# Token-major attention scores with undivided exponentials, in a kernel of pooled attention and a gated feed-forward

## The chip, the cores and the metric

The kernel runs on one core of one Trainium2 chip. The metric is device time in microseconds (us) of one execution; lower is better. The kernel before took 1031.86 us, the median of three runs (1031.65 to 1032.02).

## What is computed

Four images, each with 12288 query tokens of 128 channels and a kv map of 384 x 32 pixels. The kv map is averaged over 4 x 4 pixels to 768 rows and multiplied by `w_sr`; the result serves as key and as value.

```
kv_pool = kv.reshape(B, H//4, 4, W//4, 4, C).mean(axis=(2, 4))
k = v = kv_pool.reshape(B, -1, C) @ w_sr            # 768 rows an image
a = softmax(q @ k.T / sqrt(C))
x = (a @ v).reshape(B*N, C)                         # 49152 tokens, 128 channels
out = (maximum(x @ w_gate, 0) * (x @ w_val)) @ w_out   # d_ff = 1536
```

The feed-forward has no bias and its gate is a relu, so a positive factor on a token's row of x goes through it squared. The attention may therefore leave out its division by the sum of exponentials, if the output row is multiplied by the squared inverse of the sum.

## The kernel before, in words

The tokens are cut into 96 tiles of 512 (`T`), 24 to an image. A tile passes through five stages, each in another iteration of the outer loop (line 610), whose index is k:

- Scores (`scores`, line 290), tile k: for each of the six chunks of 128 keys, one matmul with the keys stationary and 512 tokens moving gives a bank of scores, keys on partitions. ScalarE takes its exponential into `aT` (line 295).
- Values (`values`, line 297), tile k - 1: for each chunk and each block of 128 tokens, `aT` is stationary and the values, with one more column of constants, are moving: 24 matmuls of 129 columns (line 305). The extra column is the sum of exponentials, scaled. VectorE takes its reciprocal (line 313) and multiplies (line 321); the result `x16` has tokens on partitions, and a DMA transpose (`x_turn`, line 329) turns it into `xT`, channels on partitions.
- Feed-forward, tile k - 3 (`LAG`): for each of the twelve blocks of 128 features, a value product (`value_proj`, line 374, copied to `val` by ScalarE, line 378) and a gate product (`gate_proj`, line 385). VectorE takes the relu of the gate and multiplies it by `val` in one instruction (line 388) into `hT`.
- Output product, tile k - 4 (`out_proj`, line 407): twelve matmuls into one bank. VectorE transposes that bank in blocks of 32 x 32 (line 415), GpSimd scales by a constant (line 423), and four DMAs of 64 KB store it from SP's queue (line 634).

All inner work is interleaved by a loop over 12 steps, in which each step issues one output product, one value product, a score chunk or four value matmuls, and one gate product. PSUM is one pool of eight banks taken in turn (line 85).

The first four tiles (`LEAD`) go another way, in an opening whose order is written out by hand (`OPENING`, `ENGINES`): their values are stationary, their exponentials stay undivided, and their outputs are scaled by squared inverse sums (line 421) from a matmul with ones.

Beside this, for images 2 to 4, SP loads kv in the last half of the image before, GpSimd pools it (lines 194 to 202), VectorE transposes blocks, SP places them through DRAM, TensorE projects them (line 259), and a DMA transpose gives the values (line 284). Queries are loaded by GpSimd's queue with a cast to fp16 (line 114) and turned by a DMA transpose of 2048 columns for four tiles (line 124).

Of the kernel before, what the change touches and what calls it, by code (L numbers as in the profile page):

```python
# [16 lines left out]
def kernel(  # L17
# [41 lines left out]
    LEAD = GRP  # L59
    qk_scale = 1.0 / math.sqrt(C)  # L60
# [5 lines left out]
        a0:p b0:p p0:p kvT1:a key1:a val1:a a2:p kvT2:a kvT3:a kvT4:a key4:a cast0:p qT1:a  # L66
        cast2:a cast4:p cast5:p xT3:a
    """.split())
    OPENING = """
        T1.0 T1.1 cast1 a0 T1.3 b0 T1.2 kvT1 p0 cast2 pj1 T0.3 cast3 key1 cast0 T0.p kvT0 qt2 a2  # L70
        gate22 W0 W1 cast4 qT4 wo cast5 qT5 qt1 vt1 qt3 qT2 pj0 T3.0 qT1 val1 S1.1 key0 qt0 S2.0
        S2.1 T3.1 V1.1 qT3 qT0 S1.0 S0.1 vt0 b2 val0 S3.1 S0.0 T3.2 V2.1 V0.1 T3.3 kvT3 S3.0
        V1.0 pj3 c2 p2 T2.p kvT2 key3 V0.0 S1.3 vt3 pj2 S3.3 key2 val3 S2.3 V2.0 V1.3 a4 S0.3 a5
        S1.2 S3.2 S2.2 T4.2 p4 b5 T4.p vt2 V0.3 V2.3 T4.3 val2 kvT4 S0.2 c5 p5 V2.2 pj4 V1.2
        T5.p key4 kvT5 S1.4 vt4 S0.4 val4 pj5 S2.4 V0.2 V1.4 key5 S0.5 V0.4 vt5 val5 S3.4 S2.5
        V2.4 S1.5 V0.5 S3.5 U0 xT0 V1.5 v0.2 U1 xT1 R v0.4 V2.5 xT2 v0.5 v0.3 g0.2 v0.0 V3.3
        g0.4 V3.4 v0.1 V3.5 v0.6 g0.3 g0.5 v0.7 v0.10 g0.0 v0.11 g0.10 V3.2 S4.5 S4.2 g0.1 V3.0
        v0.8 S4.0 g0.6 g0.11 v0.9 g0.8 V3.1 xT3 g0.7 S4.4 g0.9
    """.split()
    SUMS = [{"a": [0, 1], "b": ["s", 2]}, {}, {"a": [0, 1], "b": ["s", 2], "c": ["s", 3]}, {}, {"a": [0, 1]}, {"a": [0, 1], "b": ["s", 2], "c": ["s", 3]}]  # L80
# [4 lines left out]
    psum = ctx.enter_context(tc.tile_pool(name="psum", bufs=8, space=bass.MemoryType.PSUM))  # L85

    def bank(shape, dtype=FP32):
        return psum.tile(shape, dtype, tag="bank", name="bank_ps")
# [38 lines left out]
    def q_load_pair(i):  # L127
        q32 = work.tile([128, 2, NS, C], FP32, tag="q32", bufs=2, name="q32")
        nc.sync.dma_start(  # L129
            q32, q[0, i * T : (i + 2) * T, :].rearrange("(p i s) c -> p i s c", i=2, s=NS)  # L130
        )
        for n in range(2):
            q32s[i + n] = q32[:, n]

    def q_load_tile(i):
        q32 = work.tile([128, T], FP32, tag="o_t", bufs=2, name="q32_late")
        nc.sync.dma_start(
            q32, q[0, i * T : (i + 1) * T, :].rearrange("(t j s) c -> j t (s c)", j=4, s=NS)
        )
        q32s[i] = q32.rearrange("p (s c) -> p s c", s=NS)  # L140
# [17 lines left out]
    def q_turned(i):  # L158
        copy_on(f"qT{i}", qTs[0][:, i * NS : (i + 1) * NS, :], q_banks.pop(i))
# [16 lines left out]
    def kv_load(b, pair, lines=range(r), queues=(nc.sync,)):  # L176
        if (b, pair) not in kv_in:
            kv_in[b, pair] = work.tile([128, r, 2, r, C], FP32, tag="kv_in", bufs=3, name="kv_in")
# [4 lines left out]
        for dh in lines:  # L183
            queues[dh % len(queues)].dma_start(  # L184
                parts[:, dh].rearrange("p h dw c -> p (h dw c)"), rows[dh]
            )
# [3 lines left out]
    def pool_pixels(eng, b, pair, h):  # L190
        parts = kv_in[b, pair]
        s2 = work.tile([128, 2, r, C], FP32, tag="kv_s2", bufs=1)
        for i in range(2):
            eng.tensor_tensor(s2[:, i], parts[:, 2 * i, h], parts[:, 2 * i + 1, h], op=ALU.add)  # L194
# [9 lines left out]
    def line(chunk, dh):  # L204
        return kv_in[0, chunk // 2][:, dh, chunk % 2]
# [26 lines left out]
    def turned(name, chunk):  # L232
        kvT = work.tile([128, 128], FP32, tag="kvT_chunk", bufs=3, name="kvT_chunk")
        copy_on(name, kvT, kv_Ts[chunk])
# [8 lines left out]
    def keep_keys(name, jc):  # L243
        pr, engine = key_ps.pop(jc), engine_of(name)
# [9 lines left out]
    def keep_chunk_values(name, jc):  # L254
        copy_on(name, kv16[:, 0, jc, C : 2 * C], value_ps.pop(jc))

    def project(b, pair):
        pr = bank([128, 4, 2, 32])
        nc.tensor.matmul(pr, w_sr_f32, kv_Ts.pop((b, pair)), start=True, stop=True)  # L259
        nc.vector.tensor_scalar(  # L260
            kv16[:, b, 2 * pair : 2 * pair + 2, 0:C].rearrange("c h (i p) -> c h i p", p=32),
            pr.rearrange("c i h p -> c h i p"), 1.0 / (r * r), None, op0=ALU.mult,
        )

    def turn_blocks(b, pair):

        blocks = work.tile([128, 4, 2, 32], FP32, tag="kv_blocks", bufs=2)
# [22 lines left out]
    def scores(k, jc):  # L290
        if k not in aTs:
            aTs[k] = work.tile([128, NJC, T], FP16, tag="aT", bufs=5, name="aT")
        s_ps = bank([128, T])
        nc.tensor.matmul(s_ps, kv16[:, k // NST, jc, 0:C], qT_of(k), start=True, stop=True)  # L294
        nc.scalar.activation(aTs[k][:, jc, :], s_ps, AF.Exp, scale=qk_scale)  # L295

    def values(k, jc, half):
        if jc == 0:
            x_banks[k, half] = bank([128, 2, C + 1])
            if half == 0:  # L300
                x16s[k] = work.tile([128, NS, C], FP16, tag="x16", bufs=3, name="x16")
        x_ps = x_banks[k, half]
        for i in range(2):
            s = 2 * half + i
            nc.tensor.matmul(  # L305
                x_ps[:, i, :], aTs[k][:, jc, s * 128 : (s + 1) * 128],
                kv16[:, k // NST, jc, C : 2 * C + 1],
                start=(jc == 0 and i == 0), stop=(jc == NJC - 1), skip_group_check=True,
            )

    def keep_sums(k, half):
        rinvs[k, half] = work.tile([128, 2, 1], FP32, tag="rinv", bufs=4, name="rinv")
        nc.vector.reciprocal(rinvs[k, half], x_banks[k, half][:, :, C : C + 1])  # L313

    def keep_values(k, half, engine=nc.vector):
        x_ps, rinv = x_banks.pop((k, half)), rinvs.pop((k, half))
        if engine is nc.scalar:
            for i in range(2):
                nc.scalar.mul(x16s[k][:, 2 * half + i, :], x_ps[:, i, 0:C], rinv[:, i])
        else:  # L320
            nc.vector.tensor_tensor(  # L321
                x16s[k][:, 2 * half : 2 * half + 2, :], x_ps[:, :, 0:C],
                rinv.to_broadcast([128, 2, C]), op=ALU.mult,
            )

    def x_turn(k):
        x16 = x16s.pop(k)
        xT = work.tile([128, NS, 128], FP16, tag="xT", bufs=5, name="xT")
        nc.sync.dma_start_transpose(xT, x16.rearrange("p s c -> p (s c)"))
        xTs[k] = xT.rearrange("c s p -> c (s p)")  # L330

# [12 lines left out]
    def lead_kept(name, k):  # L344
        xTs[k] = work.tile([128, NS, 128], FP16, tag="xT", bufs=5, name="xT").rearrange("c s p -> c (s p)")
        copy_on(name, xTs[k], x_banks.pop(k))
# [12 lines left out]
    def lead_scales():  # L359
        turned = work.tile([128, NS * 4, 32], FP32, tag="o_sb", bufs=3, name="sums_turned")  # L360
        nc.vector.transpose(turned.rearrange("p x m -> p (x m)"), x_banks.pop("sums"))
# [9 lines left out]

    def value_proj(k, fb):
        va_ps = bank([128, T])
        nc.tensor.matmul(  # L374
            va_ps, wv16[:, fb * 128 : (fb + 1) * 128], xTs[k], start=True, stop=True
        )
        val = work.tile([128, T], FP16, tag="val", bufs=6, name="val")
        nc.scalar.copy(val, va_ps)  # L378
        vals[k, fb] = val

    def gate_proj(k, fb):
        if k not in hTs:
            hTs[k] = work.tile([128, NFB, T], FP16, tag="hT", bufs=3, name="hT")
        g_ps = bank([128, T])
        nc.tensor.matmul(  # L385
            g_ps, wg16[:, fb * 128 : (fb + 1) * 128], xTs[k], start=True, stop=True
        )
        nc.vector.scalar_tensor_tensor(  # L388
            hTs[k][:, fb, :], g_ps, 0.0, vals.pop((k, fb)), op0=ALU.max, op1=ALU.mult
# [21 lines left out]
    def out_turn(k):  # L411
# [3 lines left out]
        nc.vector.transpose(o_t, o_banks.pop(k))  # L415
# [3 lines left out]
        if k < LEAD:  # L419
            scale = lead_scale[:, k].rearrange("t (s j o) -> t s j o", s=NS, o=1)  # L420
            nc.gpsimd.tensor_tensor(to, o_by, scale.to_broadcast([128, NS, 4, 32]), op=ALU.mult)  # L421
        else:
            nc.gpsimd.tensor_scalar(to, o_by, 1.0 / X_SCALE**2, None, op0=ALU.mult)  # L423
# [19 lines left out]
    def out_scale(k, engine, own, o_ps=None):  # L443
        if k not in o_sbs:
            o_sbs[k] = work.tile([128, NS, 128], FP32, tag="o_sb", bufs=3, name="o_sb")
        o_sb, o_ps = o_sbs[k][:, own], o_ps if o_ps is not None else o_banks[k]
        if engine is nc.scalar:
            nc.scalar.mul(o_sb, o_ps, 1.0 / X_SCALE**2)
        else:
            nc.vector.tensor_scalar(o_sb, o_ps, 1.0 / X_SCALE**2, None, op0=ALU.mult)  # L450
# [51 lines left out]
    nc.sync.dma_start(w_sr_f32, w_sr)  # L502
    q_load_pair(2)
    q_load_pair(0)
    kv_load(0, 1)
    kv_load(0, 2)
    q_load_tile(4)
    q_load_tile(5)
# [18 lines left out]
    fill(4)  # L527
# [4 lines left out]
    def open_step(word):  # L532
# [44 lines left out]
        elif head == "v":  # L577
            value_proj(*at)
        elif head == "g":
            gate_proj(*at)  # L580
        elif head == "W":
# [19 lines left out]
    for word in OPENING:  # L601
# [4 lines left out]
    out_moves, moves = [], []  # L606


    last = NT + LAG - 1
    for k in range(LEAD, last + 1):  # L610
# [10 lines left out]
        for step in range(NFB):  # L621
            kO, kF = k - LAG - 1, k - LAG
            half, i = divmod(step // 2, NJC // 2)
            if 0 <= kO:
                out_proj(kO, step)
                if step == NFB - 1 and kO < NT - 3:
                    out_moves = out_turn(kO)
                elif step == NFB - 1 and k < last:
                    out_scale(kO, nc.vector, slice(0, NS))
                    out_store(kO, slice(0, NS))  # L630
            if 2 <= step < 10:
                for _ in range(2):
                    if out_moves:
                        nc.sync.dma_start(*out_moves.pop())
            if kF < NT:
                value_proj(kF, step)
            if step % 2 == 0:
                if k < NT and (k, step // 2) not in done:
# [60 lines left out]
```

## Time and profile before

| | |
|---|---|
| median of three runs | 1031.86 us |
| the profiled execution's own time | 1031.71 us |
| its span in the profile | 1029.9 us |
| TensorE busy | 1023.6 us (99%), 6508 matmuls |
| VectorE, ScalarE busy | 909.3 us each (88%) |
| GpSimd busy | 288.0 us (28%) |
| DMA, hardware queue of SP and software queue of GpSimd | 38.1% and 11.5% of 16 engines' span |

The profile is of one execution. Its span leaves out 1.8 us around it that the run's time has. Busy time is the union of an engine's instructions, which overlap on TensorE and ScalarE; so a busy share near 100% says less than the distance between starts.

### The profile page before, as it was taken

The page shows a single profiled execution, that of the slowest core. Times are in us where ns is not written, and L with a number is a line of the kernel's source. Part 1 is how long each engine was busy: PE and PEld are TensorE (multiplying, and loading weights), DVE is VectorE, ACT ScalarE, POOL GpSimd, SP SyncE. Part 2 cuts the span into 40 slices and gives each one's busy share as a digit, 9 for nine tenths or more (in the row PEclk, how much of TensorE's full clock was granted, in tenths as well). Part 3 has the DMA queues.
Part 4 walks back from the last instruction along what each step waited for, and adds up shares of the span by engine and source line. Part 5 has one row for each costly group of instructions (what it writes and reads, how often), then busy time and mean ns, then how long its engine had stood idle before and what let it go on. Part 6 is the DMA issues. An engine that isn't in the chain of part 4 may idle for free.

```text
span 1029.9 us, 19910 instructions
## 1 busy us (share of the span) xinstructions
PE 1023.6 (99%) x6508; PEld 541.1 (53%) x6508; DVE 909.3 (88%) x1666; ACT 909.3 (88%) x1742; POOL 288.0 (28%) x311
## 2 busy tenths in 40 slices
PE   8999999999999999999999999999999999999998
PEld 5455555555555555555555555555555555555555
DVE  3889898998989898998889898989898888989898
ACT  5988888888888898888898888888888898888887
POOL 4402156511221124742112122664121211111110
PEclk9999999999999999999999999999999999999999
DMA  8936386362652657826345167572552433513122
GB/s 320 116 52 80 100 184 142 78 92 39 88 69 49 74 125 158 169 57 88 54 64 88 32 88 144 146 163 58 84 77 43 73 58 62 87 32 66 33 43 51
DMA packets 327807, 93.33 MB, mean 91 GB/s; under 512 B 307480, under 2 KB 320664, under 8 KB 327704
## 3 DMA queue, kind: packets, MB, share of 16 engines
q1 hardware_dynamic: 312584, 77.97, 38.1%
q0 software_dynamic: 14688, 12.98, 11.5%
q10 hardware_dynamic: 432, 1.11, 0.3%
q8 instruction: 51, 0.84, 0.3%
q14 instruction: 52, 0.43, 0.2%
HBM read 53.94 MB, written 26.35 MB: 78 GB/s over the span
## 4 chain that ended last, share of the span: by engine, by line
PE 98%; DMA 1%; SPq 0%; DVE 0%; issue 0%; ACT 0%; ACTq 0%
PE bank_ps L374 24%; PE bank_ps L385 24%; PE bank_ps L407 23%; PE bank_ps L305 12%; PE bank_ps L294 12%; DMA q<-in_q_dram 1%; PE bank_ps L393 1%; PE bank_ps L339 1%; PE bank_ps L259 0%; PE bank_ps L227 0%; PE bank_ps L241 0%; PE bank_ps L353 0%; SPq L184 0%; DVE q L98 0%; SPq L129 0%; SPq L502 0%
## 5 line engine op out<-in xcount | busy, mean ns | idle before, releaser
L388 DVE SCALAR_TENSOR_TENSOR hT<-bank_ps,val 128x512 f16<-128x512 f32 x1152 | 757.2, 686 | 90.5 <-ACT val L378 70.4
L378 ACT CAST val<-bank_ps 128x512 f16<-128x512 f32 x1152 | 677.6, 589 | 103.0 <-PE bank_ps L374 99.9
L374 PE MATMUL bank_ps<-xT,wv 128*128 128x512 f16 x1152 | 436.3, 379 | 0.0
L385 PE MATMUL bank_ps<-xT,wg 128*128 128x512 f16 x1152 | 436.3, 379 | 0.0
L407 PE MATMUL bank_ps<-hT,wo 128*128 128x512 f16 x1116 | 423.0, 379 | 0.0
L295 ACT ACTIVATE aT<-bank_ps 128x512 f16<-128x512 f32 x576 | 344.9, 603 | 1.6 <-PE bank_ps L294 1.6
L423 POOL TENSOR_SCALAR o_sb<-o_t 128x512 f32<-128x512 f32 x89 | 132.6, 1489 | 664.6 <-DVE rinv L313 633.3
L305 PEld LDWEIGHTS <-aT 128*128 128x128 f16 x2208 | 170.6, 98 | 130.2
L294 PE MATMUL bank_ps<-qT,kv 128*128 128x512 f16 x576 | 216.6, 379 | 0.0
L305 PE MATMUL bank_ps<-kv,aT 128*128 128x129 f16 x2208 | 215.3, 220 | 0.0
L374 PEld LDWEIGHTS <-wv 128*128 128x128 f16 x1152 | 112.7, 98 | 133.4 <-DMA xT<-x 0.4
L385 PEld LDWEIGHTS <-wg 128*128 128x128 f16 x1152 | 112.7, 98 | 67.9
L407 PEld LDWEIGHTS <-wo 128*128 128x128 f16 x1116 | 109.2, 98 | 66.0 <-issue 0.2
L294 PEld LDWEIGHTS <-kv 128*128 128x128 f16 x576 | 56.2, 98 | 66.8 <-DVE kv L248 0.6
L321 DVE TENSOR_TENSOR x<-bank_ps,rinv 128x256 f16<-128x256 f32 x184 | 78.1, 425 | 6.5
L415 DVE STREAM_TRANSPOSE o_t<-bank_ps 128x512 f32<-128x512 f32 x93 | 65.6, 706 | 0.0
L114 POOL DMA_DIRECT2D q<-in_q_dram x84 | 46.3, 558 | 0.4 <-ACT xT L96 0.4
L194 POOL TENSOR_TENSOR s<-kv_in 128x512 f32<-128x512 f32 x36 | 44.9, 1267 | 0.0
L313 DVE RECIPROCAL rinv<-bank_ps 128x2 f32<-128x2 f32 x184 | 26.7, 145 | 0.0
L196 POOL TENSOR_TENSOR s<-s 128x512 f32<-128x512 f32 x18 | 22.8, 1267 | 1.4
L198 POOL TENSOR_TENSOR c<-s 128x256 f32<-128x256 f32 x18 | 13.1, 727 | 1.4
L421 POOL TENSOR_TENSOR o_sb<-o_t,lead_scale 128x512 f32<-128x512 f32 x4 | 4.2, 1048 | 32.3 <-DVE rinv L313 16.2
(68 smaller groups left out, 131.5 us busy)
## 6 DMA issues: line engine op xcount, KB each, us to landing
kv_in<-in_kv_dram SPq DMA_DIRECT2D x46, 512.0 KB, 6.8
out_dram<-o_sb SPq DMA_DIRECT2D x353, 64.0 KB, 2.2
q<-in_q_dram POOLq DMA_DIRECT2D x84, 128.0 KB, 4.6
xT<-x SPq DMA_TRANSPOSE x92, 2.5
out_dram<-o_sb SPq DMA_DIRECT2D x80, 16.0 KB, 1.5
placed<-blocks SPq DMA_DIRECT2D x9, 128.0 KB, 2.7
kvT<-placed SPq DMA_DIRECT2D x36, 32.0 KB, 1.9
kv_in<-in_kv_dram ACTq DMA_DIRECT2D x2, 512.0 KB, 7.5
```

What stands on the lines that cost most here:

```text
L114: nc.gpsimd.dma_start(q16[32 * j : 32 * (j + 1)].rearrange("t (i s) c -> t i s c", i=GRP), rows[j])
L294: nc.tensor.matmul(s_ps, kv16[:, k // NST, jc, 0:C], qT_of(k), start=True, stop=True)
L295: nc.scalar.activation(aTs[k][:, jc, :], s_ps, AF.Exp, scale=qk_scale)
L305: nc.tensor.matmul(x_ps[:, i, :], aTs[k][:, jc, s * 128 : (s + 1) * 128], kv16[:, k // NST, jc, C : 2 * C + 1], start=(jc == 0 and i == 0) ...
L321: nc.vector.tensor_tensor(x16s[k][:, 2 * half : 2 * half + 2, :], x_ps[:, :, 0:C], rinv.to_broadcast([128, 2, C]), op=ALU.mult,)
L374: nc.tensor.matmul(va_ps, wv16[:, fb * 128 : (fb + 1) * 128], xTs[k], start=True, stop=True)
L378: nc.scalar.copy(val, va_ps)
L385: nc.tensor.matmul(g_ps, wg16[:, fb * 128 : (fb + 1) * 128], xTs[k], start=True, stop=True)
L388: nc.vector.scalar_tensor_tensor(hTs[k][:, fb, :], g_ps, 0.0, vals.pop((k, fb)), op0=ALU.max, op1=ALU.mult)
L407: nc.tensor.matmul(o_banks[k], wo16[:, fb, :], hTs[k][:, fb, :], start=fb == 0, stop=fb == NFB - 1)
L415: nc.vector.transpose(o_t, o_banks.pop(k))
L423: nc.gpsimd.tensor_scalar(to, o_by, 1.0 / X_SCALE**2, None, op0=ALU.mult)
```

## The change

From the fifth tile on, the scores are made token by token: a block of 128 queries is stationary and all 768 keys are moving, in two matmuls of 512 and 256 columns, into a tile of two banks (`wide`). One ScalarE instruction takes the exponential of 768 columns and sums the row (`accum_out`). SP turns each block by a DMA transpose of 768 columns into `aT`. Two iterations later (before: one) the values are stationary and `aT` moves: six matmuls of 512 columns give `xT` directly, which VectorE copies from the bank; there is no division, no `x16` and no x transpose. The row sums are inverted on VectorE and squared on GpSimd for two tiles at a time, spread over partitions by 16 small copies, and GpSimd multiplies the outputs by them in place of the constant.

```diff
+    def score_block(k, s):
+        ...
+        s_ps = s_banks[s] = wide.tile([128, 1024], FP32, tag="wide", name="wide_ps")
+        qT = qTs[k // GRP][:, k % GRP * NS + s, :]
+        for j0, j1 in ((0, 4), (4, NJC)):
+            nc.tensor.matmul(
+                s_ps[:, j0 * 128 : j1 * 128], qT, kv16[:, b, j0:j1, 0:C], start=True, stop=True
+            )
+    def exp_block(k, s):
+        nc.scalar.activation(
+            a16s[k][:, s, :], s_banks.pop(s)[:, 0:J], AF.Exp, scale=qk_scale,
+            accum_out=a_sums[k // 2][:, k % 2, s : s + 1],
+        )
+    def invert(k):
+        ...
+        nc.vector.reciprocal(inverse, a_sums.pop(k // 2))
+        ...
+        nc.gpsimd.tensor_tensor(square, inverse, inverse, op=ALU.mult)
+    def spread_scales(k, j):
+        ...
+        for b in range(4):
+            nc.gpsimd.tensor_copy(
+                to[32 * b : 32 * (b + 1), :, :, j], squares[k // 2][32 * j : 32 * (j + 1)]
+            )
+    def a_turn(k, s0, s1):
+        aT = aTs[k].rearrange("k j t -> k (j t)").rearrange("k (x p) -> k x p", p=128)
+        nc.sync.dma_start_transpose(
+            aT[:, s0 * NJC : s1 * NJC], a16s[k][:, s0:s1, :].rearrange("p s j -> p (s j)")
+        )
+    def values(k, jc):
+        ...
+        aT = aTs[k].rearrange("k j t -> k (j t)").rearrange("k (s j p) -> k j s p", s=NS, j=NJC)
+        nc.tensor.matmul(
+            x_banks[k], kv16[:, k // NST, jc, C : 2 * C], aT[:, jc],
+            start=first, stop=x_left[k] == 0,
+        )
+    def keep_values(k):
+        ...
+        nc.vector.tensor_copy(xTs[k], freed(x_banks.pop(k)))
```

The loop over 12 steps gives way to a written order. A letter is a kind of work, a number its block: s score block, e exponential and its transpose, x value matmul, k (in `kA`) the copy to `xT`, v and y the feed-forward's value product and its copy, g and h the gate product and the product into `hT`, o output product, `oT` the output's transpose and scaling, r the inversion, and tb, P, pk the kv work.

```diff
+    STEADY = """
+        v10 s0 o0 y10 e0 v1 y1 o1 o2 o3 v0 g1 s1 o4 v2 tb y0 v9 o5 o6 e1 h1 g0 g9 y2 g10
+        o7 s2 h0 y9 g2 h10 v7 o8 h9 o9 v3 o10 o11 h2 g7 v8 e2 x1 y7 g8 s3 r oT x5 y3 g3
+        y8 v6 x4 h7 x2 x0 v5 x3 v4 h8 e3 h3 y6 P g5 y5 v11 g11 kA pk g4 y4 h5 y11 g6 h6
+        h11 h4
+    """.split()
...
-        for step in range(NFB):
...
+        kO, kF, kV = k - LAG - 1, k - LAG, k - 2
+        for word in STEADY if k < last else LAST:
+            if head == "o":
+                out_proj(kO, n)
+                for queue in (nc.gpsimd, nc.sync):
+                    if out_moves and n >= 2:
+                        queue.dma_start(*out_moves.pop())
```

The same list holds in iterations that lack a stage: its words are then passed over. The last iteration has an order by block (`LAST`). Banks are named by hand: `bank` takes the one freed longest ago out of eight, and out of six from shortly before the opening's end; the other two become `wide`. The output DMAs are shared between GpSimd's queue and SP's.

The opening has another order and other engine choices; the scores of tile 4 that it held are no longer in it, the pair of query tiles 0 and 1 is loaded ahead of the pair 2 and 3, tiles 4 and 5 are loaded in four DMAs each, and three warming matmuls stand in place of four. Buffers of `kv_in` go from three to two, of `aT` from five to four, of `xT` from five to four; new are four of `a16`, which also hold the last kv lines of the first image.

## The prediction

> **What bounds the kernel now.** I began with the page's busy shares and its chain of waits, and went on to the groups of instructions with shapes kept apart, the timeline of single engines in the middle of the run, and the issue times of the DMA queue.
>
> ```profile
> PE 1023.6 (99%) x6508; PEld 541.1 (53%) x6508; DVE 909.3 (88%) x1666; ACT 909.3 (88%) x1742; POOL 288.0 (28%) x311
> ...
> PE 98%; DMA 1%; SPq 0%; DVE 0%; issue 0%; ACT 0%; ACTq 0%
> ```
>
> The chain that ended last is TensorE for 98%. A busy matmul row proves little, because matmuls overlap (379 ns each, though a new one starts every 216 ns). So the starts decide:
>
> ```profile
> 501.57 0.39 PE L305 MATMUL bank_ps<-kv,aT 128*128 128x129 f16 x4
> 501.80 0.38 PE L385 MATMUL bank_ps<-xT,wg 128*128 128x512 f16 x1
> ...
> 503.10 0.38 PE L374 MATMUL bank_ps<-xT,wv 128*128 128x512 f16 x1
> 503.31 0.39 PE L305 MATMUL bank_ps<-kv,aT 128*128 128x129 f16 x4
> ```
>
> Two groups of value products are 1.74 us apart, with seven 512-column matmuls between: 7 x 0.216 = 1.51, and the group of four 129-column ones fills the other 0.226 (56.5 ns each). No room is left. From 37.52 (first L407) to 1023.68 (last tile's output) the counted matmuls at these prices come to about 985.7 of 986.2 us. The middle is a TensorE stream without stalls, 10.42 us a tile. The others:
>
> ```profile
> L388 DVE SCALAR_TENSOR_TENSOR hT<-bank_ps,val 128x512 f16<-128x512 f32 x1152 | 757.2, 686 | 90.5 <-ACT val L378 70.4 <-PE bank_ps L374 1.5
> L378 ACT CAST val<-bank_ps 128x512 f16<-128x512 f32 x1152 | 677.6, 589 | 103.0 <-PE bank_ps L374 99.9 <-DVE o_t L415 0.4 <-DVE rinv L313 0.3
> L295 ACT ACTIVATE aT<-bank_ps 128x512 f16<-128x512 f32 x576 | 344.9, 603 | 1.6 <-PE bank_ps L294 1.6
> ```
>
> ```profile
> 499.17 0.59 ACT L378 CAST val<-bank_ps 128x512 f16<-128x512 f32 x1 [0.17 <-PE bank_ps L374]
> 499.66 0.60 ACT L295 ACTIVATE aT<-bank_ps 128x512 f16<-128x512 f32 x1
> 500.14 0.59 ACT L378 CAST val<-bank_ps 128x512 f16<-128x512 f32 x1
> 500.91 0.59 ACT L378 CAST val<-bank_ps 128x512 f16<-128x512 f32 x1 [0.17 <-PE bank_ps L374]
> ...
> 508.49 2.47 DVE L388 SCALAR_TENSOR_TENSOR hT<-bank_ps,val 128x512 f16<-128x512 f32 x4
> ```
>
> ScalarE starts a new evacuation every 0.487 us: 18 a tile are 8.77 us, and it waits for TensorE in the rest. VectorE starts one of the L388 products every 0.617: 7.40 a tile, with the transpose (0.63) and two normalisations (1.0) about 9.0. Both have under 1.7 us to spare.
>
> **What the Trainium skill says.** (1) "TensorE: Matmul & The Clock Gate", section "Wait — 56ns, not 53.3ns?": warm matmuls start N / 2.4 GHz + 2.5 ns apart, 215.7 ns at 512 columns. The trace agrees: 216, and 56.5 for 129 (56.3 by the formula). So 256 columns should take 109 ns. (2) "PSUM — Partial Sum Buffer", section "The four PSUM rules": an output fits one bank of 512 fp32. Hence a 768-column score block takes two matmuls and two banks. (3) "ScalarE: Activation LUTs", section "What ACT_TABLE_LOAD costs": 0.833 ns per element, neighbours overlapping by 93 ns. The trace shows 0.10 overlap. (4) "DMA: Bandwidth & Descriptors", section "Latency and other measured facts": 261 GB/s for transposes. This trace is slower (below), and its number is used.
>
> **The change part by part**, for the 92 tiles from the fifth on.
>
> TensorE. Scores: six of 512 columns (1.296 us) become four pairs of 512 + 256: 4 x (0.216 + 0.109) = 1.300. Values: 24 x 56.5 = 1.356 become 6 x 0.216 = 1.296. Net -0.056 a tile, and with the formula's bare 56.3 -0.050. For 92 tiles that is -4.6 to -5.2; I take **-5.0**. The period goes from 10.42 to 10.37. Weight loads drop from 66 to 50 a tile and lie beside running matmuls, as now.
>
> ScalarE. Twelve casts stay (5.84). Six exponentials (2.92) become four of 768 columns: 603 + 256 x 0.833 = 816 ns, less 0.116 overlap, 0.70 each, 2.80. No row here shows the new accumulated row sum. Bounds: 0 if it rides along, 0.30 if it is a further small instruction like the 202 ns ACTIVATE on one column (L512) with its overlap lost too. I take 0.2 each. Sum 9.44 of 10.37: hidden by TensorE, until the readout reaches (10.37 - 8.64) / 4 = 0.43.
>
> VectorE. Gone: two reciprocals and two L321 products (about 1.0). New: one xT cast like L98's 689 ns (0.62 in a row) and a small reciprocal per two tiles (0.07). Sum 8.72, 0.3 less, hidden.
>
> GpSimd. The output scaling goes from 1489 ns (L423) to the broadcast form, 1048 (L421). Added per two tiles: a square and 16 small copies (16 took 3.68 here). Two output DMAs a tile move here from SP at 0.56 each (L114's issue). Sum about 1.05 + 1.9 + 1.1 + 0.55 for q = 4.6, and 5.0 more in the 18 image tiles that pool kv: 9.6, still under a period. Its lateness is covered by two o_t buffers; without them VectorE's transpose would wait.
>
> SP and the DMA engines. The x transpose (512 columns, 1.21 us of issue) goes; four of 768 columns come.
>
> ```profile
> L329 SPq DMA_TRANSPOSE xT<-x x92: 1189/1213/3097, 57.6 to 1009.4; - x92
> ...
> L124 SPq DMA_TRANSPOSE qT<-q x22: 1912/3868/5914, 43.9 to 928.4; - x22
> ...
> 45.00:46.00 1.00, 1.00 (x6) 0.45 (x5) 1.00 (x3) 0.88 (x3) 0.00 (x0) 1.00 0.99 193
> 46.00:47.00 1.00, 1.00 (x6) 0.49 (x5) 1.00 (x2) 0.94 (x3) 0.00 (x0) 1.00 1.17 217
> ```
>
> Columns of the first two: issue time min/median/max in ns. The undisturbed 2048-column transpose took 1.91 us of issue and, in the windows from 43 to 48 (two shown; DMA share is the last but one number), 2.9 us of all 16 engines, 180 GB/s. Interpolated, 768 columns take 1.3 us of SP and 1.1 us of the engines. SP per tile: 4 x 1.3 + 2 outputs x 0.62 + qT 3.9 / 4 = 7.4 of 10.37; up to 5.5 more in alternate image tiles (kv loads, placing, value turns). DMA engines: today's queues took 38.1 + 11.5%, 511 us; less 92 x 0.78, plus 92 x 4.4: 844, 82%. What waits behind these: in SP's order each a_turn waits for its exponential, and outputs, qT and kv moves queue behind. The products need the result late: the last exponential stands at about 70% of iteration k, the first product at 60% of k + 2, nearly two periods (19 us) against a landing of 2.5 to 9 us. So all of this is costed at nothing; the cover is that distance.
>
> Banks. Two of eight now belong to one score block, refilled only after its exponential has read it; v and g products have four banks beside o and x. In STEADY 7, 9 and 11 matmuls (1.5 us or more) lie between one block and the next, against about 1.4 for the matmuls' end (0.4), one cast ahead in ScalarE's queue and the exponential with its readout: a refill should just find its banks read.
>
> Tiles that are not full. STEADY is laid for a whole tile. Iterations 4 and 5 carry no values: TensorE 9.08 us, but ScalarE 9.44, at least 0.37 lost in each. Iterations 96 to 98 have no scores, and o4 needs h4, VectorE's last product of the iteration before, only 14 words earlier. Following the words with the durations above I find 0.5 to 0.8 lost in each of the five: 0.8 to 3.6 in all; I take **+2.3**. Before lost nothing there.
>
> Opening. The pair of q tiles needed first is loaded first: pairs landed at 10.76 and 12.05, the first score stood at 14.24, so up to 0.7 earlier. Against it, with all eight banks until its last words but four exponentials moved into iteration 4, the same order-following ends the opening 0.4 earlier with 0.86 less work done. Bounds -0.7 to +0.9: I take **0**. End: ScalarE's last scale reads a pointer operand, **+0.1**.
>
> Sum: -5.0 + 2.3 + 0 + 0.1 = -2.6 against the profiled execution's 1031.71 (span 1029.9 and 1.8 around it): **1029.1**. The median of the runs is 1031.86, 0.15 higher, so the forecast isn't moved for that. About 0.2% (2.06 us) is what a measurement can tell from no change.
>
> **Rivals.**
> B, slower: ScalarE becomes the bound through the accumulator. For: it is priced by nothing here, and ScalarE has only 0.93 left at my value. Against: it needs over 0.43 a block, twice a bare small instruction. At 0.5: 5.84 + 4 x 1.2 = 10.64, +0.27 for some 90 tiles, +24: about 1053.
> C, slower: SP and the DMA engines. For: 82% mean load, and qT's issue doubles from 1.9 to 3.9 when others load. It decides where a transpose costs SP over 2.0 us. At 2.4: 9.6 + 2.2 = 11.8, +1.4 a tile: about 1160. Against: x transposes mostly kept to 1.21.
> D, no gain: single words wait for a bank. At 0.05 a tile the saving is eaten: about 1034.
> E, the change doesn't save what it says: strided moving operands (aT in four runs, kv in runs of 128) stream slower than contiguous ones. At 10% on twelve matmuls, +0.26 a tile: 1053. No operand of the trace is read so in the middle of the run, so this stays open.
> F, faster than my sum: short tiles and opening cost nothing: about 1026.8.
>
> **Chances.** Forecast 0.60 (its own range 1027.3 to 1031.5: two thirds of it beyond -2.06), B 0.08, C 0.09, D 0.14, E 0.02, F 0.07. Faster: 0.40 + 0.07 = 0.47. Within 0.2%: 0.19 + 0.05 from D = 0.24. Slower: 0.01 from the forecast, 0.09 from D, and B, C and E, 0.29. The range from 1026.0 to 1041.0 leaves out B, C and E, 0.19.
>
> **What would show it.** Right: period 10.37, TensorE 97% or more of the chain, the xT copy and 768-column exponentials hidden, ScalarE near 93% busy, few waits of TensorE, those at about 40 to 60 and after 1000 us. Wrong: an exponential pitch over 1.1 us, a value product waiting for DMA, SP busy throughout, or a period over 10.42.

## The result and the profile after

The changed kernel takes 1061.57 us in the median (1060.13 to 1064.8), the kernel before 1031.76: a ratio of 1.0294 [1.0275, 1.0313], slower. The forecast was 1029.1. The profiled execution has a span of 1060.7 us against 1029.9, so 30.8 us have to be found. First, the page's busy shares (busy us, share of the span, instructions) and its chain of waits:

```profile
PE 1028.4 (97%) x5034; PEld 490.5 (46%) x5034; DVE 864.2 (81%) x1434; ACT 921.6 (87%) x1931; POOL 527.8 (50%) x1309
...
PE 93%; DMA 3%; DVE 2%; SPq 1%; ACT 1%; issue 0%; ACTq 0%; DVEq 0%
```

TensorE still carries the chain, but with 93% where it had 98%; DMA (3%), VectorE (2%) and SP's queue (1%) have the rest. The engines that the change loads are not full. The groups with shapes kept apart (busy us, mean ns of one, idle time before and its releaser) say the same of ScalarE and VectorE:

```profile
L462 DVE SCALAR_TENSOR_TENSOR hT<-bank_ps,val 128x512 f16<-128x512 f32 x1152 | 728.1, 680 | 114.8 <-PE bank_ps L454 91.4
L450 ACT CAST val<-bank_ps 128x512 f16<-128x512 f32 x1152 | 630.8, 596 | 76.8 <-PE bank_ps L443 56.7
L352 ACT ACTIVATE a<-wide_ps 128x768 f16<-128x768 f32 x368 | 301.9, 820 | 44.1 <-PE wide_ps L347 44.0
L352 ACT ACTIVATION_READ_ACCUMULATOR a<-wide_ps 128x1 f32 x368 | 75.8, 206 | 0.0
```

Most of their idle time is waiting for TensorE. The timeline of the middle (start, duration) shows the period on VectorE's xT copies, one a tile, and what an exponential costs on ScalarE:

```profile
503.37 0.81 ACT L352 ACTIVATE a<-wide_ps 128x768 f16<-128x768 f32 x1 [0.17 <-PE wide_ps L347]
504.08 0.20 ACT L352 ACTIVATION_READ_ACCUMULATOR a<-wide_ps 128x1 f32 x1
504.17 2.27 ACT L450 CAST val<-bank_ps 128x512 f16<-128x512 f32 x4
...
839.01 0.69 DVE L397 CAST xT<-bank_ps 128x512 f16<-128x512 f32 x1 [0.35 <-PE bank_ps L389]
849.37 0.69 DVE L397 CAST xT<-bank_ps 128x512 f16<-128x512 f32 x1 [0.36 <-PE bank_ps L389]
859.74 0.69 DVE L397 CAST xT<-bank_ps 128x512 f16<-128x512 f32 x1 [0.36 <-PE bank_ps L389]
```

The copies are 10.365 us apart, where the kernel before needed 10.42. The steady tile is as forecast. The loss is elsewhere, and the list of waits (us in all, times, longest) names the place:

```profile
PE wide_ps L288 <- DMA kvT<-placed: 22.5, 5, 7.7
PEld wide_ps L288 <- issue: 21.6, 3, 8.2
...
SPq L699 <- DMA placed<-blocks: 36.2, 9, 7.9
```

L288 is the projection of a pair of kv chunks, nine in the run. Its operand kvT has gone from VectorE's blocks through `placed` in DRAM (L311) and back in four loads (L699), all on SP. Nine intervals between xT copies hold a projection. Undelayed such an interval is 10.80 us; here they are 20.68, 10.80, 11.16, then 20.60, 10.79, 11.68, then 18.78, 12.19, 12.73: **32.2 us** too much. The first pair of each image has 27.7 of them. One such pair, in the timelines of VectorE, SP and TensorE:

```profile
163.35 0.43 DVE L306 STREAM_TRANSPOSE blocks<-kv_s 128x256 f32<-128x256 f32 x1
...
155.90 6.06 SPq L379 DMA_TRANSPOSE aT<-a  x3
162.05 1.30 SPq L723 DMA_DIRECT2D out_dram<-o_sb  x2
163.44 5.28 SPq L379 DMA_TRANSPOSE aT<-a  x4
168.82 0.58 SPq L213 DMA_DIRECT2D kv_in<-in_kv_dram  x1
169.83 1.27 SPq L723 DMA_DIRECT2D out_dram<-o_sb  x2
171.16 0.90 SPq L213 DMA_DIRECT2D kv_in<-in_kv_dram  x1
172.16 0.60 SPq L311 DMA_DIRECT2D placed<-blocks  x1
180.70 0.78 SPq L699 DMA_DIRECT2D kvT<-placed  x2
...
188.18 1.19 PE L288 MATMUL wide_ps<-kvT,w_sr_f 128*128 128x256 f32 x2 [7.02 <-DMA kvT<-placed]
```

VectorE makes the blocks at 163.35. SP issues their write 8.8 us later, because it is still working off older transposes, outputs and kv loads: from 121.72 to 172.76, nearly five tiles, no gap between two of its issues is over 0.5 us, where in the tile before there were gaps of 1.4 and 2.5. Then it stands until 180.70 for the write to land, and everything behind stands with it. TensorE would have reached the projection at 181.0 and gets it at 188.2. The same chain in the kernel before:

```profile
163.55 0.43 DVE L268 STREAM_TRANSPOSE blocks<-kv_s 128x256 f32<-128x256 f32 x1
...
165.86 0.59 SPq L273 DMA_DIRECT2D placed<-blocks  x1
...
173.58 1.75 SPq L660 DMA_DIRECT2D kvT<-placed  x4
...
180.47 0.59 PE L259 MATMUL bank_ps<-kvT,w_sr_f 128*128 128x256 f32 x2
```

There the write left 2.3 us after its blocks. The last load, issued at 174.90, took 4.8 us to land (the longest of the 36, whose median is 1.9), so only 0.8 us were left before the projection. From the blocks to the last landing the chain now takes 24.7 us in place of 16.1. Of the 8.6 more, 6.5 are the later write, 0.8 its landing (8.5 against 7.7) and 1.2 the loads, the last two of which now stand behind a transpose and a kv load.

Why SP falls behind only there is in the table of windows, two tiles each (columns: window, its length, busy us of PE, PEld, DVE, ACT and POOL, granted clock, DMA share, GB/s). Of after:

```profile
124.00:145.00 21.00, 21.00 (x103) 9.95 (x102) 17.95 (x30) 19.29 (x41) 14.60 (x32) 1.00 1.09 213
155.00:176.00 21.00, 21.00 (x103) 9.88 (x101) 18.15 (x31) 19.29 (x42) 18.07 (x35) 1.00 1.01 208
240.00:261.00 21.00, 21.00 (x103) 9.93 (x102) 17.95 (x31) 19.29 (x41) 7.74 (x23) 1.00 0.75 128
```

Of before:

```profile
124.00:145.00 21.00, 21.00 (x134) 11.04 (x133) 18.84 (x36) 18.91 (x37) 7.99 (x9) 1.00 0.95 191
155.00:176.00 21.00, 21.00 (x138) 11.09 (x135) 19.08 (x36) 18.91 (x37) 12.99 (x15) 1.00 0.52 138
240.00:261.00 21.00, 21.00 (x134) 11.02 (x133) 18.84 (x36) 18.92 (x37) 5.12 (x6) 1.00 0.25 39
```

While the next image is loaded and placed, the DMA engines are full after the change (1.01 to 1.09) and had room before it at the time of the placing (0.52). In tiles without image work they have a quarter to spare even after it (0.75). A transpose then takes SP longer to issue, as the instructions of the aT tile show (min/median/max ns):

```profile
L379 SPq DMA_TRANSPOSE aT<-a x368: 1209/1239/6187, 40.1 to 1024.8; - x184
```

The 17 that SP issued from 121.72 to 168.72 took 29.5 us, 1.74 each: 8.5 more than at 1.24, about as much as the whole lag of 8.8. Four of them (2.03, 6.19, 1.78 and 3.04) have 8.1 of the 8.5, and the longest, from 130.60, comes right behind four kv loads issued from 122.98 to 129.16. The one qT turn among them took 3.96, about as in the kernel before, where the median was 3.87.

The account, against before: steady tiles 90 x -0.055 = -5.0; projections +32.2; iterations 4, 5 and 96 to 98 +2.9 (four times 9.73 us between outputs or xT copies where TensorE alone would need 9.07, and an estimated 0.3 in the rest); the opening +1.6. Together they give +31.7, which is 0.9 more than the measured 30.8; the opening is the least certain of them.

The 32.2 are not waiting alone. In and after this stall TensorE's clock is granted at half, as smaller windows show (the clock is again the third number from the end):

```profile
184.00:188.00 4.00, 0.00 (x0) 0.00 (x0) 0.00 (x0) 0.00 (x0) 1.76 (x2) 0.50 0.90 247
188.00:190.00 2.00, 1.82 (x4) 0.95 (x5) 0.52 (x2) 0.00 (x0) 0.00 (x0) 0.50 1.13 199
190.00:192.00 2.00, 2.00 (x6) 0.76 (x5) 1.05 (x2) 0.62 (x2) 1.65 (x2) 0.50 1.27 268
...
194.00:196.00 2.00, 2.00 (x11) 0.98 (x10) 0.69 (x1) 1.61 (x5) 0.22 (x1) 1.00 0.52 95
```

Of the 9.9 us that this projection lost, 7.2 are the wait. The trace has the clock at half from 183.27 to 193.51; the other 2.7 fit the 5.3 us of matmuls from 188.18 on at twice their spacing. The Trainium skill, "TensorE: Matmul & The Clock Gate", section "HAM oscillation — how this bites in real kernels", says that the clock drops to half in gaps of TensorE over about 3.4 us. This gap of 7.0 us agrees, though the clock fell already 2.1 us after the end of the last matmul (181.16).

### The profile page after: what moved, and what is told of

Its sections match the earlier page's. It is cut to its first block, busy times and chain, and to the rows that moved or that the text cites. A ratio compares the mean times of both kernels' runs of the same rounds, so it can differ in the third digit from the quotient of the medians.

```text
span 1060.7 us, 17991 instructions
## 1 busy us (share of the span) xinstructions
PE 1028.4 (97%) x5034; PEld 490.5 (46%) x5034; DVE 864.2 (81%) x1434; ACT 921.6 (87%) x1931; POOL 527.8 (50%) x1309
## 4 chain that ended last, share of the span: by engine, by line
PE 93%; DMA 3%; DVE 2%; SPq 1%; ACT 1%; issue 0%; ACTq 0%; DVEq 0%
PE bank_ps L454 23%; PE bank_ps L443 23%; PE bank_ps L482 22%; PE wide_ps L347 11%; PE bank_ps L389 11%; DMA kvT<-placed 1%; DVE hT L462 1%; DMA placed<-blocks 1%; DMA kv_in<-in_kv_dram 1%; PE bank_ps L256 1%; PE wide_ps L288 1%; ACT val L450 1%; PE bank_ps L468 1%; PE bank_ps L332 0%; SPq L699 0%
## 5 line engine op out<-in xcount | busy, mean ns | idle before, releaser
L454 PE MATMUL bank_ps<-xT,wg 128*128 128x512 f16 x1152 | 377.4, 382 | 0.7 <-DVE hT L462 0.7
L482 PE MATMUL bank_ps<-hT,wo 128*128 128x512 f16 x1116 | 347.8, 380 | 0.2 <-DVE hT L462 0.2
L352 ACT ACTIVATE a<-wide_ps 128x768 f16<-128x768 f32 x368 | 301.9, 820 | 44.1 <-PE wide_ps L347 44.0
L347 PE MATMUL wide_ps<-kv,qT 128*128 128x512 f16 x736 | 180.5, 327 | 0.0
L389 PE MATMUL bank_ps<-aT,kv 128*128 128x512 f16 x552 | 179.2, 379 | 0.0
L454 PEld LDWEIGHTS <-wg 128*128 128x128 f16 x1152 | 113.3, 98 | 126.8 <-issue 5.0
L495 POOL TENSOR_TENSOR o_sb<-o_t,scale 128x512 f32<-128x512 f32 x89 | 93.3, 1049 | 142.2 <-issue 124.2
L373 POOL COPY scale<-square 32x8 f32<-32x8 f32 x736 | 142.1, 193 | 28.5
L723 POOL DMA_DIRECT2D out_dram<-o_sb x216 | 135.1, 628 | 19.1 <-POOL o_sb L495 13.7
L347 PEld LDWEIGHTS <-qT 128*128 128x128 f16 x736 | 72.3, 98 | 88.3 <-issue 2.2
L397 DVE CAST xT<-bank_ps 128x512 f16<-128x512 f32 x92 | 63.6, 692 | 32.3 <-PE bank_ps L389 32.3
L352 ACT ACTIVATION_READ_ACCUMULATOR a<-wide_ps 128x1 f32 x368 | 75.8, 206 | 0.0
```

The source lines that it names most:

```text
L347: nc.tensor.matmul(s_ps[:, j0 * 128 : j1 * 128], qT, kv16[:, b, j0:j1, 0:C], start=True, stop=True)
L352: nc.scalar.activation(a16s[k][:, s, :], s_banks.pop(s)[:, 0:J], AF.Exp, scale=qk_scale, accum_out=a_sums[k // 2][:, k % 2, s : s + 1],)
L373: nc.gpsimd.tensor_copy(to[32 * b : 32 * (b + 1), :, :, j], squares[k // 2][32 * j : 32 * (j + 1)])
L389: nc.tensor.matmul(x_banks[k], kv16[:, k // NST, jc, C : 2 * C], aT[:, jc], start=first, stop=x_left[k] == 0,)
L454: nc.tensor.matmul(proj_banks["g", k, fb], wg16[:, fb * 128 : (fb + 1) * 128], xTs[k], start=True, stop=True,)
L482: nc.tensor.matmul(o_banks[k], wo16[:, fb, :], hTs[k][:, fb, :], start=fb == 0, stop=fb == NFB - 1)
```

## The experiments

The theory, called Q in the expectations, is that words behind SP's backlog at image tiles, the kv write and loads above all, come too late. Against it stood that the transposes themselves are late for the value products, that the DMA engines and not SP's time are the limit (rival D; it may be what makes SP's issues long in the first place), and that ScalarE's accumulator costs something (rival B). The edits are against the changed kernel, that of before_load against the kernel before; ratios are to the kernel before, to be read against 1.0294.

### late: more distance for the kv chain

```diff
-        pair, odd = divmod(at - 6, 2)
+        pair, odd = divmod(at - 8, 2)
...
-        at = k % NST - (NST - NJC - 6)
+        at = k % NST - (NST - NJC - 8)
...
-                pair, odd = divmod(at - 4, 2)
+                pair, odd = divmod(at - (4 if head == "tb" else 6), 2)
```

> The projection of a kv pair, its copy and the value turns stand two iterations later after the placing, and the whole kv pipeline of an image starts two iterations earlier; nothing else is changed. Theory Q (the placing transfers come late through SP's queue, and TensorE waits for them at the nine projections): the waits of some 32 us in all vanish, 1061.6 becomes 1029 to 1031, tile period stays 10.365. Rival D (the 16 DMA engines are too loaded, everything that lands is late): the waits go too, but products wait for transposes elsewhere, over 1035. Rival S (the loss lies in short tiles, opening or clock, and the projection only collects it): it stays over 1050.

Measured: 1050.53, 1.0182 [1.0167, 1.0197]. The projections no longer wait, but the waits of this kernel show the value products in their place:

```profile
PE bank_ps L389 <- DMA aT<-a: 12.9, 7, 4.1
PEld L389 <- issue: 12.4, 18, 3.4
PEld L389 <- DMA aT<-a: 11.4, 4, 4.6
```

So the narrow form of Q, that only the kv words come late, missed. It is what rival D forecast: over 1035, with products waiting for transposes. The number alone would fit S too, but the waits are not where S has them. With its landing, a transpose is now later than the 19 us that lie ahead of a product. In late the kv write leaves up to 18.2 us after its blocks, in the changed kernel at most 10.9; this suggests that there the stalls at the projections let SP catch up.

### pairs: half as many transposes of twice the width

```diff
-                    if head == "e":
-                        a_turn(k, n, n + 1)
+                    if head == "e" and n % 2:
+                        a_turn(k, n - 1, n + 1)
```

> Two transposes of 1536 columns a tile in place of four of 768: same bytes, half the instructions. Theory Q (SP's issue time is what backs up): a tile's transposes cost SP about 2 x 1.7 = 3.4 in place of 5.0 us, over the four tiles in which it backs up some 6 of the 9 to 11 us of lateness, and the projection waits shrink from 32 us to 5 to 15: 1035 to 1045. Rival D (bytes on the DMA engines): unchanged, 1059 to 1064.

Measured: 1031.74 (1029.06 to 1033.68), 0.9999 [0.9991, 1.0008], better than I expected. The bytes are the same; the excess at the projections fell from 32.2 to 2.6 us. A transpose of 1536 columns costs SP 1.46 us where two of 768 cost 2.48:

```profile
L379 SPq DMA_TRANSPOSE aT<-a x184: 1274/1462/4568, 40.0 to 993.3; - x184
```

The write after the first pair's blocks now leaves 2.75 us after them (161.50 to 164.25), not 8.8. At the second pairs it still leaves 8.0 to 8.5 us after them, and no projection waits. The DMA engines are as busy as in the changed kernel (1.21 and 1.03 against 1.09 and 1.01):

```profile
124.00:145.00 21.00, 21.00 (x103) 9.94 (x102) 17.95 (x30) 19.29 (x42) 14.91 (x32) 1.00 1.21 207
155.00:176.00 21.00, 21.00 (x103) 9.88 (x101) 18.16 (x31) 19.29 (x42) 17.94 (x36) 1.00 1.03 213
```

So full engines alone don't make the loss; what fell is SP's time.

### quad: one transpose a tile

```diff
-                    if head == "e":
-                        a_turn(k, n, n + 1)
+                    if head == "e" and n == 3:
+                        a_turn(k, 0, 4)
```

> One transpose of 3072 columns a tile, after its fourth exponential; same bytes. By pairs (1.46 us for 1536 columns against 1.24 for 768) one instruction of about 1.9 to 2.4 us undisturbed in place of 5.0. Count theory: waits vanish, 1029 to 1031. If long transposes hold the ring and what is queued behind them (placing, loads, outputs) comes later, waits of 5 us or more return: over 1034.

Measured in three executions: 1035.91 (1030.76 to 1035.95), 1.0024 [1.0004, 1.0044], the second of the two expectations. Fewer still is no better: 3072 columns hold SP for 4.41 us (median), so the saving over two pairs (2.92) is gone.

### chain_pool and kv_pool: parts of the kv work on GpSimd's queue

```diff
-        nc.sync.dma_start(placed, blocks.rearrange("p j h c -> p (j h c)"))
+        nc.gpsimd.dma_start(placed, blocks.rearrange("p j h c -> p (j h c)"))
...
-                nc.sync.dma_start(*moves.pop())
+                nc.gpsimd.dma_start(*moves.pop())
```

> The write of the kv blocks to DRAM and the four loads back are issued by GpSimd's queue in place of SP's. Theory Q: the write is issued within 1 to 2 us of VectorE's transpose in place of 9 to 11, the projection waits vanish, 1029 to 1034. Rival D: the write still takes 4 to 8 us to land, but the lead then hides it; waits under 5 us, so only the landing time tells. Rival P (GpSimd itself is late in the image tiles, with the copies of the scales and the output transfers): no gain or worse, over 1055, as the loads then queue behind pooling.

Measured: 1047.01, 1.0144 [1.0127, 1.0161], between Q's range and P's. The wait for kvT is gone, but GpSimd now stands at L699, on its own engine, where pooling and output scaling come next, and TensorE waits for hT (L454, 12.5 us in 7 times). That the late scaling held VectorE up, and so hT, is what the order of the words suggests; it wasn't tested.

```diff
-            kv_load(b, at // 2, [step // 3])
+            kv_load(b, at // 2, [step // 3], (nc.gpsimd,))
```

> The kv loads of images 2 to 4 (12 of 512 KB an image) are issued by GpSimd's queue in place of SP's; same bytes. Theory Q: SP is relieved of some 3 us in every second image tile, the lateness of the placing falls from about 10 to 4 to 7 us, the waits from 32 to 5 to 20 us: 1035 to 1050. Rival D: same bytes on the same engines, 1059 to 1064.

Measured: 1040.86 (1037.63 to 1046.0), 1.0094 [1.0063, 1.0125], as Q expected. Taking SP's issues of the kv loads away, with all bytes left in place, brings back some two thirds of the loss; the loads also start at other moments, so this is not the issue time alone.

### pairs_kvpool and best: both cures together

> Both reliefs of SP at once: transposes of two blocks, and kv loads on GpSimd's queue. Theory Q: what is left in pairs (1.65, 0.83 and 0.11 us of projection waits above the projection's own 0.43) goes, so 1031.7 becomes 1028.5 to 1030; the DMA engines' share stays about 80%. Rival D (engine load): the residue is from landing times and stays, 1031 to 1033. Rival P (GpSimd becomes late): over 1034.

Measured: 1047.07 (1043.08 to 1049.56), 1.0144 [1.0118, 1.0169]. Two cures of SP's queue are worse together than either alone, which a count of SP's issues cannot explain. The number is in P's range, but TensorE waits for kvT at three projections, as before. SP's transposes now took up to 8.1 us to issue, and the first pair's chain shows what that does:

```profile
L379 SPq DMA_TRANSPOSE aT<-a x184: 1274/1461/8079, 40.2 to 1004.7; - x184
...
162.15 0.36 SPq L311 DMA_DIRECT2D placed<-blocks  x1
...
167.02 5.55 SPq L379 DMA_TRANSPOSE aT<-a  x1
172.62 1.35 SPq L699 DMA_DIRECT2D kvT<-placed  x2
```

The write leaves 0.46 us after its blocks (161.69), so SP's lag is cured. But the last two loads stand behind a transpose of 5.55 us and take 11.5 and 11.9 us to land. GpSimd had issued three kv loads from 166.03 to 167.12, around the start of that transpose; in pairs SP issued its own at 161.32, 163.53, 172.69 and 174.76. So the likely reason is that the loads, no longer spaced by SP's own order, reach the same 16 engines at once, and SP's queue pays. That agrees with the Trainium skill, "DMA: Bandwidth & Descriptors", section "Issuing engines are not separate DMA queues": another issuing engine saves only the issue time.

The kernel "best" adds to this another order of words for the tiles that are not full:

> As pairs_kvpool, and the iterations that lack a stage (the fifth tile's, and the last three) run in an order by feature block, with each copy and product right behind its matmul, and with all eight banks for the last three, where no scores are left. Theory: the short iterations' loss is one of order and banks, 0.66 + 0.66 + 0.3 + 0.6 us in after for these; about 2 us of it goes: 1026.5 to 1028. Rival: the loss is the plain load of ScalarE and VectorE there, no change against pairs_kvpool within 0.4.

Measured: 1043.49, 1.012 [1.0099, 1.0141]; it carries the same stalls.

### no_qload: less for the DMA engines, the same for SP

```diff
+    kept = {}
...
+        if g > 3:
+            q16s[g] = kept[g % 2]
+            return
...
+        kept[g % 2] = q16
```

> After, but the queries of tiles 16 and up are not loaded: GpSimd's queue leaves those transfers out and the same two buffers are turned again (the output is then of other queries). SP issues exactly what it does in after; the DMA engines lose some 10% of span of work. If SP's own issuing is what backs up (its count of instructions), the waits stay: 1058 to 1063. If SP is held back by the engines (its ring drains too slowly), they shrink to 5 to 15 us: 1032 to 1045.

GpSimd's queue leaves out the query loads from the fifth group of tiles on. Measured: 1050.87, 1.019 [1.0176, 1.0204]; between the two expectations. SP issues all that it did, yet the excess at the projections falls from 32.2 to 19.8 us. So load that SP has no part in lengthens its backlog, and is not all of it.

### before_load: the transposes alone, in the kernel before

```diff
-            aTs[k] = work.tile([128, NJC, T], FP16, tag="aT", bufs=5, name="aT")
+            aTs[k] = work.tile([128, NJC, T], FP16, tag="aT", bufs=4, name="aT")
...
+                    for at_step, c in ((2, 0), (4, 1), (8, 2), (10, 3)):
+                        if step == at_step and k > GRP:
+                            spare = work.tile([128, 6, 128], FP16, tag="spare", bufs=4, name="spare")
+                            nc.sync.dma_start_transpose(
+                                spare, aTs[k].rearrange("p j t -> p (j t)")[:, c * 768 : (c + 1) * 768]
+                            )
```

> The kernel before with four unused transposes of 768 columns a tile added on SP's queue behind its exponentials (and four aT buffers in place of five for the room). Its x transposes stay, and its output stores stay on SP, so SP has more to issue than in after: 4 x 1.24 + 1.21 + 4 x 0.62 + 1 for qT = 9.7 us in a tile of 10.42. Theory Q: SP falls behind in the image tiles and probably everywhere; TensorE waits for xT or at the projections: 1055 to 1150. Rival (the loss needs the change's own order or its shared two-bank tile): within 3 us of 1031.7.

Measured: 1188.96, 1.1536 [1.151, 1.1561], more than was expected. The old kernel, with its own scores and exponentials, stalls when its SP and DMA engines carry four such transposes a tile:

```profile
PEld L374 <- DMA xT<-x: 93.4, 40, 9.6
PE bank_ps L374 <- DMA xT<-x: 74.7, 33, 9.1
PEld bank_ps L259 <- issue: 41.8, 9, 6.1
PE bank_ps L259 <- DMA kvT<-placed: 37.7, 9, 5.7
```

It stalls at the projection (here L259), and also at xT, which has less distance than the values. SP has more to do here than after the change (its x transposes and all outputs stayed), so the size isn't comparable; the kind is.

### spread: the same work, thinner

```diff
-        if step % 3 == 1 and 0 <= at < NJC and at % 2 == 0:
-            kv_load(b, at // 2, [step // 3])
+        if step == 1 and 0 <= at < 2 * NJC:
+            kv_load(b, at // 4, [at % 4])
...
-        at = k % NST - (NST - NJC - 6)
+        at = k % NST - 6
```

Pooling, placing and projection follow at one pair in four tiles (they were at one in two); the distance from blocks to projection is the same.

> The kv pipeline of an image is stretched: one line of 512 KB is loaded a tile in place of four in every second, so a pair takes four tiles and not two; same transfers, same four transposes of 768 columns, and the same distance from the placing to its projection. Theory L (momentary overload: in six tiles of 24 loads, pooling traffic and transposes together ask more of SP's queue and the DMA engines than a tile's 10.37 us): the waits of 32 us vanish, 1028.5 to 1031. Rival N (SP's queue is overfull in every tile and the placing is only where it shows): the waits stay over 10 us, 1040 or more.

Measured: 1033.02 (1028.71 to 1036.75), 1.0009 [0.9997, 1.0022]. Not one transpose less, nothing on another queue, and in the profiled execution (span 1026.9) all nine projection intervals are 10.79 to 10.92 us; SP's longest transpose took 3.1 us to issue, not 6.2. This is the clearest evidence that the loss is a matter of demand per tile. The profiled execution is the fastest of the twelve, though. The scatter of 8 us and a median above the expectation say that the others still lose time; where they do isn't known.

### pairs_noacc: rival B

To the edit of pairs is added:

```diff
+                nc.gpsimd.memset(a_sums[k // 2], 768.0)
...
-            accum_out=a_sums[k // 2][:, k % 2, s : s + 1],
```

> Pairs without the row sums: the exponential's accumulator output is left out, and outputs are scaled by a constant sum of 768. Theory: the 195 ns readouts lie in ScalarE's slack, so the tile period stays 10.365 and the time within 1 us of pairs (1031.7). Rival B (the readout costs TensorE): the period falls by up to 0.05 and the time to 1027 or less.

Measured in 18 executions: 1031.09, 1.0000 [0.9991, 1.0009]; pairs has 0.9999. 75.9 us of readouts taken from ScalarE change nothing: B falls.

### best2: pairs, the thinner kv work and the short tiles

The edits of pairs and spread, and in iterations 4 and 96 to 98

```diff
-        for word in STEADY if k < last else LAST:
+        if k == NT:
+            scoring.close()
...
+            usable[0] = 8
+        for word in SHORT if k == LEAD or k >= NT else STEADY:
```

with SHORT an order that takes the blocks in turn, and the score banks given to the other tiles once no scores are left.

> Pairs, the stretched kv pipeline, and the order by feature block with eight banks for the fifth tile's iteration and the last three. Theory: no projection waits (pairs had 2.6 us left), and about 1.5 to 2 us of the short iterations' loss gone: 1026.5 to 1028. If short iterations lose by plain engine load: 1029.

Measured: 1028.18 (1026.45 to 1028.94), 0.9959 [0.9946, 0.9973]: 0.4% faster than the kernel before. From the first xT copy to the end it needs 997.5 us (28.92 to 1026.4) and spread 999.7 (27.16 to 1026.9); of the difference 2.0 lie after the last full tile's xT copy (33.1 against 35.1) and 0.4 around iteration 4. The page of best2:

```profile
PE 1018.9 (99%) x5034; PEld 488.8 (48%) x5034; DVE 863.4 (84%) x1434; ACT 921.5 (90%) x1931; POOL 528.0 (51%) x1309
...
PE 97%; ACT 1%; DMA 1%; DVE 1%; issue 0%; ACTq 0%; DVEq 0%
```

## Why the prediction was wrong, by its own steps

**TensorE, -5.0: right.** 10.365 against 10.42. With it D and E fall: there is no room for a wait for banks, nor for slower strided operands, in that period.

**ScalarE, hidden: right.** The exponential took 812 ns alone (816 estimated). The readout is an instruction of its own, 195 ns, but exponential and readout together hold ScalarE for 0.80 us (503.37 to 504.17), so it adds 0.1, not 0.2, and is far from the 0.43 of rival B.

**VectorE and GpSimd, hidden: right** in the changed kernel; GpSimd is at 50%.

**SP and the DMA engines, nothing: this step failed.** Its prices were right: 1.24 us of issue (1.3 estimated), 79% of the engines (82%). The conclusion, "So all of this is costed at nothing; the cover is that distance", failed twice. The distance of 19 us was that of the transposes, and the step names the kv moves queued behind them without asking how long those may wait: in the kernel before, the first pair's last load landed 0.8 us ahead of its projection. In place of nothing, the projections cost 32.2 us. And 82% was a mean over the run. The same paragraph had 7.4 + 5.5 = 12.9 us of SP for a period of 10.37 in alternate image tiles, over by 2.5, and left it at that. With the 7.4 of the tile between, the mean is 10.15, so only 0.2 us a tile were left to catch up; and with the engines full, the issues stretched to 1.74 on the mean.

None of its four signs of being wrong appeared. They were asked of exponentials, value products, SP throughout and the period, not of the words that stand behind the transposes. One sign of being right did fail: TensorE has 93% of the chain, not 97% or more.

**Rival C: the right resource, the wrong shape.** It asked whether a transpose costs SP over 2.0 us throughout. The median never did. The loss is a backlog at nine places, so 32 us and not 130.

**Banks, nothing: right**, since scores hardly wait (L347's weight loads 2.2 us in 8 times).

**Tiles that are not full, +2.3: 2.9**, within its bounds. The working there doesn't come out, though: 0.5 to 0.8 in each of five is 2.5 to 4.0, not 0.8 to 3.6. **F** asked for these tiles and the opening at nothing.

**Opening, 0: +1.6** in this execution, beyond its bound of +0.9. The clock accounts for about that much. All twelve changed kernels have this opening. In six profiled executions (this one, quad, chain_pool, best, no_qload, best2) the trace has the clock at half for 3.4 us from 8.0 to 9.8 on, and the first xT copy stands at 28.6 to 29.0; in the other six the clock stays full there, and the copy stands at 27.0 to 27.3. The window from 8 to 12 us, after and pairs:

```profile
8.00:12.00 4.00, 3.30 (x18) 3.30 (x19) 1.17 (x2) 0.00 (x0) 2.49 (x3) 0.65 1.04 413
...
8.00:12.00 4.00, 3.29 (x31) 2.99 (x32) 1.51 (x4) 0.00 (x0) 2.66 (x3) 1.00 1.03 411
```

At half clock 3.4 us lose 1.7. So the forecast of 0 held only for executions without it, and single executions of these kernels can differ by that much. The two profiles of the kernel before and of before_load show no half clock there; whether the fourth warming matmul, which the change left out, prevents it wasn't tested.

Not settled is how the 32.2 us divide between the number of SP's issues and the load of the engines. kv_pool and no_qload each changed mainly one of the two and each brought part back, pairs took away nearly all with the engines as full, and pairs_kvpool shows that they act on each other.

## What to carry to other kernels

A queue that is served in order needs its demand added up tile by tile, at the busiest tiles and with everything that shares it, and then the time until the due moment of every item behind the new ones, not of the new ones alone. Where a backlog shows, make fewer and larger issues (two blocks a transpose here; four were no better) or spread the bursts before moving work to another queue: the engines behind the queues are the same. A stall found at one consumer may be what keeps the next one from stalling.

## What the runs showed of the hardware that was not expected

- The issue time of a transpose on SP is no constant. For 768 columns it was 1.21 to 6.19 us (median 1.24), for 1536 columns 1.27 to 4.57 (1.46), and up to 8.08 where another queue carried the kv loads.
- It doesn't grow evenly with width: medians 1.24, 1.46 and 4.41 us for 768, 1536 and 3072 columns, and the shortest 1.21, 1.27 and 3.54.
- Reading out the accumulator shows as 195 ns after every exponential and costs ScalarE about 0.1.
- One stretch of 3.4 us at half clock in the opening came in six of twelve profiled executions and moved the first xT copy by some 1.7 us.
